# Output projection of an attention + Fourier kernel: the order of the row pairs' splits, of the normalization of the last pairs, and of the first sequence coefficients

## The chip, the cores and the metric

The kernel runs on one core of a Trainium2 chip. The metric is the device time of one execution in microseconds (us); lower is better. The time before is 2464.6 us, the median of three runs (2461.26 to 2467.86).

Five engines of the core work side by side, each through its own list of instructions in a fixed order: TensorE (PE, matrix products; its weight loads are shown apart as PEld), VectorE (DVE), ScalarE (ACT), GpSimd (POOL), and SyncE (SP), which here only issues transfers. An instruction that waits holds up everything behind it on its engine.

## The reference

Two layers, each an attention block followed by a Fourier block, on 2048 rows of 640 numbers, in 32-bit floats:

```python
def _A_ref(x, wqkv, wo):              # H = 32 heads of 20
    qkv = (x @ wqkv) ...
    scores = einsum("bhqd,bhkd->bhqk", q, k) * Dh ** -0.5
    o = einsum("bhqk,bhkd->bhqd", softmax(scores), v)
    return o... @ wo
def _B_ref(x, seq_re, seq_im, hid_re, hid_im):
    a, b = x @ hid_re.T, x @ hid_im.T
    return seq_re @ a - seq_im @ b
x = x + _A_ref(_layernorm(x), wqkv, wo)
x = x + _B_ref(_layernorm(x), ...)
x = x + _A_ref(_layernorm(x), wqkv, wo)
x = x + _B_ref(_layernorm(x), ...)
```

The change lies where `o @ wo` is added to `x` and the result is normalized for the Fourier block. This stage runs twice, once in each layer.

## The kernel before

To keep 32-bit accuracy, every operand of a product is split into a high part (a copy in a rounded format) and a low part (the rest), and a product is three matmuls: high times high, high times low, low times high (`three`, lines 95 to 97). `split` (lines 87 to 90) makes the parts: the high one on ACT (line 89) or DVE (line 87), then the low one on DVE (line 90), which needs the high one.

The projection is `Project.run`. It goes over eight **pairs** p = 0 to 7; a pair is two tiles of 128 rows whose positions are 1024 rows apart. For each pair:

- `load(p + 3)` brings the rows of x for a later pair through the SP queue; a buffer of these is free again when the store of the pair four before it has finished.
- `product(n)` for both tiles: on PE two halves of 320 columns, each of five blocks of three matmuls, so 60 matmuls for a pair, into four PSUM banks that are used in turn. DVE adds x to each half and takes the row sums (line 1006), which frees the bank. The first five tiles have their first three blocks done earlier, during attention.
- after pairs 1 and 3, `fetch` brings the attention output `o` (high and low) of the next four tiles: eight transfers on the SP queue (line 975).
- `normal(k)` for an earlier pair k (the table `LAG`): DVE writes `fold` (line 1061), out of `g` and `na`; `na` comes from ACT (`scale`, lines 1047 to 1049), where the table `SCALED` may put it ahead. For k = 2, 3, 6 and 7 the fold is added to and subtracted from that of k - 2 (line 1066), and the two results are split into `xn` (line 89 on ACT, line 90 on DVE). `xn` numbers 0 to 3 (q) are what the Fourier products read.
- `moments(p)`: the store of the pair to memory (line 1018, SP), the mean (lines 1021 and 1022, POOL), two sums of squares (line 1024, ACT), the power and the factors (lines 1026 to 1041, POOL; line 1040 writes the `nb` that `scale` needs), and `g`, the sum and difference of the two halves of a row (lines 1035 and 1036, DVE).

`normal` is a generator: it stops once after the sums of line 1066, then the run puts `moments(p)` in, and only then do the splits into `xn` follow. So ACT has `scale` of pair 3 and the squares of pair 4 in its list before the high part of xn 0.

The **Fourier products** (`accumulate`) follow with no other work between on PE: q = 0 and 1 for the first two accumulators, then q = 2, then q = 3. They read `xn` and `chl`, the split sequence coefficients. `parts(i)` splits block i of these: high on ACT (line 1209), low on DVE (line 1211). Six blocks are split during the projection, two each after pairs 3, 4 and 5. When both blocks of a load are split, the next load of coefficients (`craw`, line 1201) is issued on SP.

The order of every engine's list is the order in which the code calls these functions; nothing reorders it. POOL's and SP's lists are given by the same calls.

Of the kernel before, what the change touches and what calls it, by code (L numbers as in the profile page):

```python
# [5 lines left out]
F32 = mybir.dt.float32  # L6
# [9 lines left out]
S, D, H, DH = 2048, 640, 32, 20  # L16
# [8 lines left out]
NP = NT // 2  # L25
NQ = NT // 4
LATE = (1, 4, 6)
DONE = 3
LAG = {0: [], 1: [], 2: [0], 3: [1], 4: [2], 5: [3], 6: [4, 5]}
SCALED = {2: [1], 3: [2], 4: [3], 5: [4]}  # L30
FIRST = (0, 1, 4, 5)
HD = D // 2
TOL = 2.0 ** -32
# [5 lines left out]
def mha_fnet_kernel(ctx, tc, x_in, wqk, wv, wo, seq, hid, nat_seq, nat_hid, out):  # L39
# [44 lines left out]
    def split(hl_h, hl_l, src, vector=False):  # L84

        if vector:
            V.tensor_copy(hl_h, src)  # L87
        else:
            A.activation(hl_h, src, AF.Copy)
        V.tensor_tensor(hl_l, src, hl_h.bitcast(F32), op=OP.subtract)  # L90
# [852 lines left out]
    class Project:  # L943
# [105 lines left out]
            A.activation(dst[:, HD + 1:], g[:, HD + 1:], AF.Identity, scale=r, bias=zero[:dst.shape[0]])  # L1049

        def scale(s, p):
            a = s.na[p] = s.next.late("raw1" if p == 1 else "raw0", [D], F32, "na")
            s.scaled(a, s.g[p][:, 0], s.rs[p][:, 0, 0:1], s.nb[p][:, 0:1], s.nb[p][:, 1:2])

        def normal(s, p):
            if p not in s.na:
                s.scale(p)
            rs, g, nb, a = s.rs[p], s.g[p], s.nb[p], s.na[p]
            f = s.f[p] = s.room(f"f{p % 4}", [D], F32, "fold")
            for cols, r in ((slice(0, HD + 1), rs[:, 0, 1:2]), (slice(HD + 1, D), nb[:, 2:3])):  # L1060
                V.scalar_tensor_tensor(f[:, cols], g[:, 1, cols], r, a[:, cols], op0=OP.mult, op1=OP.add)
            if p - 2 not in FIRST:
                return
            q, t = FIRST.index(p - 2), (s.next.late("raw1", [D], F32, "fold2"), f)
            for k, op in enumerate((OP.add, OP.subtract)):
                V.tensor_tensor(t[k], s.f[p - 2], f, op=op)
            yield
            for k in range(2):
                xn = s.next.keep(f"xn{2 * q + k}", [2, D], F32R, "xn")
                s.xn[q, k] = [xn[:, 0], xn[:, 1]]  # L1070
                split(xn[:, 0], xn[:, 1], t[k])

        def run(s):
            s.ot[2] += s.heads(s.room, 2, (1,))
            s.ot.append(s.heads(s.room, 3))
            for m, part in ((0, 1), (1, 0), (1, 1)):
                s.fetch(1, m, part)
            for p in range(NP):
                if p:
                    s.load(p + 3)  # L1080
                for n in (2 * p, 2 * p + 1):
                    s.product(n)
                if p in (1, 3):
                    for m in range(2):
                        for part in range(2):
                            s.fetch(p // 2 + 2, m, part)

                parts = iter(())
                for k in LAG.get(p, [p - 1]):
                    list(parts)  # L1090
                    parts = s.normal(k)
                    next(parts, None)
                if p == 3:
                    s.next.ahead(1, (0,))
                for k in SCALED.get(p, []):
                    s.scale(k)
                s.moments(p)
                list(parts)
                if p == 3:
                    s.next.edge_sum(0)  # L1100
                    s.next.ahead(1, (1,))
                if p == 6:
                    s.next.edge_sum(1)
                    s.next.mids()
                if p == 1:
                    s.next.ahead(0)
                elif p in (4, 5):
                    s.next.ahead(p - 2)
            list(s.normal(NP - 1))

# [4 lines left out]
    class Fourier:  # L1117
# [6 lines left out]
        def weights(s, k):  # L1124
# [11 lines left out]
                split(w[:n, 0], w[:n, 1], s.raw["w", k][:n], vector=True)  # L1136

            return load, parts

        def ahead(s, n, *halves):  # L1140

            for k in range(3) if n == 0 else range(2 * n - 2, 2 * n):
                s.parts(k, *halves) if n else s.load(k)

        def edges(s, n):

# [45 lines left out]
        AHEAD = 6  # L1192
# [430 lines left out]
```

## Time and profile before

| what | us |
|---|---|
| median of three runs | 2464.6 |
| the profiled execution, its own time | 2466.32 |
| its span, first to last instruction | 2464.5 |
| PE busy in it | 2432.3 (99%) |
| ACT busy | 2116.3 (86%) |
| DVE busy | 993.8 (40%) |
| POOL busy | 529.9 (21%) |
| mean clock granted to TensorE | 0.996 |

How to read it: PE and ACT are busy in long stretches of attention, where neither is far from full. A busy PE is no proof that it runs at its peak, so short stretches have to be looked at by themselves: the projection of layer 0 lies at 1103 to 1167 us of the span, that of layer 1 at about 2324 to 2388 us. "Idle before, releaser" in the listings is how long an engine stood still before an instruction and what ended this. The granted clock is the share of TensorE's full clock in a stretch.

### The profile page before, as it was taken

The page shows a single profiled execution, that of the slowest core. Times are in us where ns is not written, and L with a number is a line of the kernel's source. Part 1 is how long each engine was busy: PE and PEld are TensorE (multiplying, and loading weights), DVE is VectorE, ACT ScalarE, POOL GpSimd, SP SyncE. Part 2 cuts the span into 40 slices and gives each one's busy share as a digit, 9 for nine tenths or more (in the row PEclk, how much of TensorE's full clock was granted, in tenths as well). Part 3 has the DMA queues.
Part 4 walks back from the last instruction along what each step waited for, and adds up shares of the span by engine and source line. Part 5 has one row for each costly group of instructions (what it writes and reads, how often), then busy time and mean ns, then how long its engine had stood idle before and what let it go on. Part 6 is the DMA issues. An engine that isn't in the chain of part 4 may idle for free. (4 is left out here: it accounts for less than half of the span.)

```text
span 2464.5 us, 43830 instructions
## 1 busy us (share of the span) xinstructions
PE 2432.3 (99%) x16350; PEld 1178.2 (48%) x16350; DVE 993.8 (40%) x2198; ACT 2116.3 (86%) x2428; POOL 529.9 (21%) x1032
## 2 busy tenths in 40 slices
PE   8999999999999999999999999999999999999998
PEld 7644444443333333349885444454433333333586
DVE  6244442234343333427763444323333232333275
ACT  6699998899999999985457989888999999999752
POOL 2012211112111212114421212211212212222143
PEclk9999999999999999999999999999999999999999
DMA  5224231223222225317552332312221222152265
GB/s 183 100 89 126 81 112 53 77 67 116 72 93 87 96 78 172 93 52 273 189 185 96 111 101 88 114 53 69 82 81 57 92 64 70 55 148 82 81 227 196
DMA packets 128228, 262.64 MB, mean 107 GB/s; under 512 B 29937, under 2 KB 54289, under 8 KB 128005
## 3 DMA queue, kind: packets, MB, share of 16 engines
q1 hardware_dynamic: 89412, 159.89, 20.1%
q0 software_dynamic: 38592, 99.85, 12.7%
q8 instruction: 132, 2.16, 0.4%
q14 instruction: 92, 0.75, 0.1%
HBM read 175.29 MB, written 84.31 MB: 105 GB/s over the span
## 5 line engine op out<-in xcount | busy, mean ns | idle before, releaser
L524 ACT ACTIVATE e<-psc 128x1024 f32<-128x1024 f32 x2048 | 1919.3, 1058 | 110.4 <-PE psc L521 98.7
L532 PE MATMUL acc<-e,v 128*32 128x512 f32 x8192 | 1034.1, 600 | 0.4 <-DVE of L539 0.4
L521 PE MATMUL psc<-stq,stk 62*128 62x512 f32 x4096 | 745.5, 445 | 2.3 <-ACT e L524 1.1
L521 PEld LDWEIGHTS psc<-stq,stk 62*128 62x128 f32 x4096 | 333.5, 184 | 704.0 <-ACT e L524 565.2
L532 PEld LDWEIGHTS acc<-e,v 128*32 128x32 f32 x8192 | 217.4, 108 | 397.0 <-issue 358.6
L102 PE MATMUL pqk<-xt,wqk 128*128 128x512 f32 x1200 | 319.5, 407 | 0.0
L553 POOL DMA_DIRECT2D o<-oh x256 | 131.4, 522 | 827.4 <-DVE oh L548 815.7
L87 DVE CAST hl<-pqk 128x512 fp32r<-128x512 f32 x64 | 44.3, 692 | 597.7 <-PE pqk L102 597.7
L102 PEld LDWEIGHTS pqk<-xt,wqk 128*128 128x128 f32 x1200 | 213.6, 188 | 83.5 <-issue 39.8
L102 PE MATMUL pv<-wv,xt 128*128 128x320 f32 x960 | 151.3, 313 | 0.0
L102 PEld LDWEIGHTS pv<-wv,xt 128*128 128x128 f32 x960 | 141.1, 188 | 15.5 <-issue 9.7
L553 POOL DMA_DIRECT2D o<-ot x256 | 128.4, 509 | 1.6 <-issue 0.8
L539 DVE STREAM_TRANSPOSE of<-acc 128x512 f32<-128x512 f32 x64 | 45.8, 715 | 198.2 <-PE acc L532 198.2
L210 POOL DMA_DIRECT2D scrq<-hl x40 | 28.3, 707 | 429.6 <-DVE hl L90 239.8
L210 POOL DMA_DIRECT2D scrk<-hl x40 | 27.8, 694 | 390.3 <-DVE hl L90 280.8
L95 PE MATMUL py<-wo,o 128*128 128x320 f32 x320 | 103.3, 323 | 8.4 <-DVE xr L1006 8.4
L216 DVE TENSOR_REDUCE top<-pn 32x1 f32<-32x512 f32 x80 | 53.5, 676 | 121.1 <-PE pn L215 120.7
L802 DVE TENSOR_REDUCE far<-cq 128x1 f32<-128x512 f32 (+5 forms) x169 | 98.5, 584 | 5.7
L96 PE MATMUL py<-wo,o 128*128 128x320 f32 x320 | 100.3, 313 | 0.0
L97 PE MATMUL py<-wo,o 128*128 128x320 f32 x320 | 100.3, 313 | 0.0
L806 DVE TENSOR_TENSOR cq<-cq 128x512 f32<-128x512 f32 (+4 forms) x166 | 96.3, 580 | 3.7 <-DMA cq<-in_nat_seq_dram 2.7
L246 DVE COPY v<-pv 128x320 f32<-128x320 f32 x32 | 15.7, 489 | 161.3 <-PE pv L102 161.3
(201 smaller groups left out, 1755.1 us busy)
## 6 DMA issues: line engine op xcount, KB each, us to landing
cq<-in_nat_seq_dram POOLq DMA_DIRECT2D x64, 512.0 KB, 5.3
scrq<-hl POOLq DMA_DIRECT2D x40, 512.0 KB, 3.2
scrk<-hl POOLq DMA_DIRECT2D x40, 512.0 KB, 3.1
stq<-scrq SPq DMA_DIRECT2D x256, 80.0 KB
stk<-scrk SPq DMA_DIRECT2D x128, 160.0 KB
o<-o SPq DMA_DIRECT2D x32, 384.0 KB
stq<-scrq SPq DMA_DIRECT2D x256, 40.0 KB
stk<-scrk SPq DMA_DIRECT2D x128, 80.0 KB
```

The lines of the kernel that those rows point to most:

```text
L95: PE.matmul(out_ap, ah, bh, start=start, stop=False)
L96: PE.matmul(out_ap, ah, bl, start=False, stop=False)
L97: PE.matmul(out_ap, al, bh, start=False, stop=stop)
L102: yield lambda i=i, j=j, k=k: PE.matmul(out_ap, a[i], b[j], start=dc == 0 and k == 0, stop=dc == ND - 1 and k == 2)
L210: G.dma_start(s.scr["qk"[k]][c * 128:(c + 1) * 128, :, tb * 512:(tb + 1) * 512], hl.bitcast(F32))
L216: V.tensor_reduce(s.top[:H, c // ND, c % ND, tb:tb + 1], p, op=OP.max, axis=AX.X)
L521: PE.matmul(p[:, i], s.k[g, kc // 8, j][r, kc % 8 * 128:(kc % 8 + 1) * 128], s.q[g, qb, j][r], start=True, stop=True)
L524: A.activation(e, p, AF.Exp, scale=SCALE)
L532: PE.matmul(s.acc[32 * j:32 * j + 32], s.a.v[kc][:, v0:v0 + 32], s.e[n, j // 2][:, j % 2], start=kc == 0, stop=kc == NT - 1, skip_group_ch ...
L553: G.dma_start(s.o[k, h * DH:(h + 1) * DH, qb * 512:(qb + 1) * 512], hl[k][32 * j:32 * j + DH])
L802: V.tensor_reduce(to, x, op=OP.max, axis=AX.X, apply_absolute_value=True)
L806: V.tensor_tensor(y, x, y, op=op)
```

## The change

The splits into `xn` now follow straight behind the sums of line 1066; `normal` is a plain function. Every pair from 2 on is normalized two pairs later (`LAG`: pair 4 behind the product of pair 6, pair 5 behind that of pair 7), and pairs 6 and 7 follow together at the end. `na` is made one pair ahead for pairs 1 to 6 (`SCALED`), pair 6's in the other of two buffers. The splits of the coefficient blocks stand in a table, `AHEAD`: blocks 0 and 1 at pair 3, 2 and 3 at pair 4, 4 at pair 5, 5 at pair 6, with the high parts always ahead of `scale` and `moments` and the low parts behind.

```diff
-LAG = {0: [], 1: [], 2: [0], 3: [1], 4: [2], 5: [3], 6: [4, 5]}
-SCALED = {2: [1], 3: [2], 4: [3], 5: [4]}
+LAG = {0: [], 1: [], 2: [0], 3: [1], 4: [2], 5: [3], 6: [4], 7: [5]}
+SCALED = {2: [1], 3: [2], 4: [3], 5: [4], 6: [5], 7: [6]}
+AHEAD = {3: (0, 1), 4: (2, 3), 5: (4,), 6: (5,)}
...
-            a = s.na[p] = s.next.late("raw1" if p == 1 else "raw0", [D], F32, "na")
+            a = s.na[p] = s.next.late("raw1" if p in (1, 6) else "raw0", [D], F32, "na")
...
                 V.tensor_tensor(t[k], s.f[p - 2], f, op=op)
-            yield
             for k in range(2):
...
-                parts = iter(())
                 for k in LAG.get(p, [p - 1]):
-                    list(parts)
-                    parts = s.normal(k)
-                    next(parts, None)
-                if p == 3:
-                    s.next.ahead(1, (0,))
+                    s.normal(k)
+                if p in AHEAD:
+                    for i in AHEAD[p]:
+                        s.next.parts(i, (0,))
                 for k in SCALED.get(p, []):
                     s.scale(k)
                 s.moments(p)
-                list(parts)
+                if p == 1:
+                    for _ in range(3):
+                        s.next.load(_)
                 if p == 3:
                     s.next.edge_sum(0)
-                    s.next.ahead(1, (1,))
+                if p in AHEAD:
+                    for i in AHEAD[p]:
+                        s.next.parts(i, (1,))
                 if p == 6:
                     s.next.edge_sum(1)
                     s.next.mids()
-                if p == 1:
-                    s.next.ahead(0)
-                elif p in (4, 5):
-                    s.next.ahead(p - 2)
-            list(s.normal(NP - 1))
+            for k in (NP - 2, NP - 1):
+                s.normal(k)
```

(`ahead`, a helper that called `load` and `parts`, is removed with it.) The lists of PE, SP and POOL stay the same in their order. Those of ACT and DVE change in the projection alone, in the same way in both layers. Line numbers of the changed kernel are one higher up to `normal` and six lower behind `run`; the names are the same.

ACT, behind pair 3's squares (`xsq`) and the sum at the row's edge (`e`), before:

```order
L1178 ACTIVATE e_11361<-c3raw 1x640
L1047 ACTIVATE na<-g,nb,ars 128x321
L1048 ACTIVATE na<-g,nb,ars 128x2
L1049 ACTIVATE na<-g,zero,ars 128x319
L1024 ACTIVATE xsq,sumsq<-xr,mean 128x640 x2
L89 ACTIVATE xn<-fold_11722 128x640
L89 ACTIVATE xn<-fold 128x640
L1209 ACTIVATE chl<-craw 128x512 x2
```

The same place in the changed kernel:

```order
L1172 ACTIVATE e_11361<-c3raw 1x640
L90 ACTIVATE xn<-fold_11722 128x640
L90 ACTIVATE xn<-fold 128x640
L1203 ACTIVATE chl<-craw 128x512 x2
L1048 ACTIVATE na<-g,nb,ars 128x321
L1049 ACTIVATE na<-g,nb,ars 128x2
L1050 ACTIVATE na<-g,zero,ars 128x319
L1025 ACTIVATE xsq,sumsq<-xr,mean 128x640 x2
```

The high parts of xn 0 and the two coefficient blocks moved ahead of pair 3's `na` and pair 4's squares.

DVE from the sums of pair 4's products to those of pair 5's, before:

```order
L1006 SCALAR_TENSOR_TENSOR xr,rowsum<-py,xr 128x320 x4
L1061 SCALAR_TENSOR_TENSOR fold<-g,ars,na 128x321
L1061 SCALAR_TENSOR_TENSOR fold<-g,nb,na 128x319
L1066 TENSOR_TENSOR fold_11722<-fold 128x640
L1066 TENSOR_TENSOR fold<-fold 128x640
L1035 TENSOR_TENSOR g<-xr 128x2x319
L1036 TENSOR_TENSOR g<-xr 128x2x319
L90 TENSOR_TENSOR xn<-fold_11722,xn 128x640
L90 TENSOR_TENSOR xn<-fold,xn 128x640
L1211 TENSOR_TENSOR chl<-craw,chl 128x512 x2
L1006 SCALAR_TENSOR_TENSOR xr,rowsum<-py,xr 128x320 x4
```

The same in the changed kernel:

```order
L1007 SCALAR_TENSOR_TENSOR xr,rowsum<-py,xr 128x320 x4
L1062 SCALAR_TENSOR_TENSOR fold<-g,ars,na 128x321
L1062 SCALAR_TENSOR_TENSOR fold<-g,nb,na 128x319
L1067 TENSOR_TENSOR fold_11722<-fold 128x640
L1067 TENSOR_TENSOR fold<-fold 128x640
L91 TENSOR_TENSOR xn<-fold_11722,xn 128x640
L91 TENSOR_TENSOR xn<-fold,xn 128x640
L1036 TENSOR_TENSOR g<-xr 128x2x319
L1037 TENSOR_TENSOR g<-xr 128x2x319
L1205 TENSOR_TENSOR chl<-craw,chl 128x512 x2
L1007 SCALAR_TENSOR_TENSOR xr,rowsum<-py,xr 128x320 x4
```

The low parts of xn 0 moved ahead of `g`; the same instructions stand between the two sets of sums.

DVE at the end of the projection, behind the sums of pair 7's products; before:

```order
L1061 SCALAR_TENSOR_TENSOR fold<-g,ars,na 128x321
L1061 SCALAR_TENSOR_TENSOR fold<-g,nb,na 128x319
L1066 TENSOR_TENSOR fold_12059<-fold 128x640
L1066 TENSOR_TENSOR fold<-fold 128x640
L1035 TENSOR_TENSOR g<-xr 128x2x319
L1036 TENSOR_TENSOR g<-xr 128x2x319
L90 TENSOR_TENSOR xn<-fold_12059,xn 128x640
L90 TENSOR_TENSOR xn<-fold,xn 128x640
```

The same in the changed kernel:

```order
L1062 SCALAR_TENSOR_TENSOR fold<-g,ars,na 128x321
L1062 SCALAR_TENSOR_TENSOR fold<-g,nb,na 128x319
L1036 TENSOR_TENSOR g<-xr 128x2x319
L1037 TENSOR_TENSOR g<-xr 128x2x319
L1062 SCALAR_TENSOR_TENSOR fold<-g,ars,na 128x321
L1062 SCALAR_TENSOR_TENSOR fold<-g,nb,na 128x319
L1067 TENSOR_TENSOR fold_12080<-fold 128x640
L1067 TENSOR_TENSOR fold<-fold 128x640
L91 TENSOR_TENSOR xn<-fold_12080,xn 128x640
L91 TENSOR_TENSOR xn<-fold,xn 128x640
```

The first fold here was pair 6's and is now pair 5's; pair 6's fold, its sums and xn 2 stand behind pair 7's `g`. Pair 7's fold and xn 3 close both lists.

More of the change, by code (lines that the diff above doesn't have):

```diff
@@ L1138, in weights @@
             return load, parts
-        def ahead(s, n, *halves):
-            for k in range(3) if n == 0 else range(2 * n - 2, 2 * n):
-                s.parts(k, *halves) if n else s.load(k)
         def edges(s, n):
```

## The prediction

> **What bounds the kernel now.** I first read the list of waits of PE, since PE and ACT carry the span and the change touches ACT and DVE only where PE runs dense products. It gives, for PE, who was waited for: us in total, times, longest.
>
> ```profile
> PE ptr L166 <- ACT xa L129: 8.7, 2, 8.3
> PE py L95 <- DVE xr L1006: 8.4, 4, 3.5
> ```
>
> Apart from the start (8.3), the only wait of weight in the program is that for line 1006, which frees the projection's PSUM banks. The timeline of PE puts it at the first product of pair 6 in both layers (start, length, what, idle before):
>
> ```profile
> 1107.80 0.41 PE L95 MATMUL py<-wo,o 128*128 128x320 f32 x1 [0.67 <-DVE xr L1006]
> ...
> 1147.68 0.57 PE L95 MATMUL py<-wo,o 128*128 128x320 f32 x1 [3.53 <-DVE xr L1006]
> 1166.92 0.40 PE L95 MATMUL pacc<-chl,xn 128*128 128x512 f32 x1
> ...
> 2367.91 0.63 PE L95 MATMUL py<-wo,o 128*128 128x320 f32 x1 [3.53 <-DVE xr L1006]
> 2387.96 0.40 PE L95 MATMUL pacc<-chl,xn 128*128 128x512 f32 x1
> ```
>
> PE stands still from 1144.15 to 1147.68, and from 2364.38 to 2367.91. The `pacc` rows are the first Fourier products; call their start F. A second loss hides in "busy". At full speed two matmuls are 0.147 us apart: 89 steps lie between these two rows, (1132.84 - 1119.78) / 89.
>
> ```profile
> 1119.78 0.31 PE L95 MATMUL py<-wo,o 128*128 128x320 f32 x1
> ...
> 1132.84 0.31 PE L97 MATMUL py<-wo,o 128*128 128x320 f32 x1
> ```
>
> So the 120 matmuls of pairs 6 and 7 need 17.6 us. They took 1166.92 - 1147.68 = 19.24 in layer 0 and 20.05 in layer 1: 1.64 and 2.45 too many. The table of short stretches says why; behind the counts of the engines stands the granted clock, then the DMA share and GB/s:
>
> ```profile
> 1108.00:1109.00 1.00, 1.00 (x8) 1.00 (x8) 0.98 (x6) 0.00 (x0) 1.00 (x3) 1.00 0.79 249
> 1147.00:1148.00 1.00, 0.32 (x1) 0.32 (x2) 1.00 (x6) 0.00 (x0) 0.47 (x2) 0.89 0.91 247
> 1151.00:1152.00 1.00, 1.00 (x8) 1.00 (x8) 1.00 (x2) 1.00 (x2) 0.00 (x0) 0.91 0.98 398
> 2366.00:2367.00 1.00, 0.00 (x0) 0.00 (x0) 1.00 (x3) 0.31 (x1) 0.91 (x3) 0.67 1.02 321
> 2373.00:2374.00 1.00, 1.00 (x8) 1.00 (x7) 0.20 (x1) 1.00 (x3) 0.34 (x2) 0.92 0.21 86
> ```
>
> The first row, behind the idle 0.67, is at full clock. Read as shares of full and half clock, the others put the fall at 1147.78 and the return at about 1151.2, and in layer 1 the fall at 2366.34 and the return at 2373.2. Half the cold time with work in it is 1.7 and 2.6, which fits the excess. The stall thus costs 3.53 + 1.64 = 5.17 in layer 0 and 3.53 + 2.45 = 5.98 in layer 1: **11.15 us together**.
>
> Why line 1006 was late is read on DVE, ACT and POOL before it:
>
> ```profile
> 1140.14 0.22 POOL L1040 TENSOR_SCALAR nb<-nb 128x1 f32<-128x1 f32 x1
> ...
> 1140.40 0.66 ACT L1047 ACTIVATE na<-g,nb,ars 128x321 f32<-128x321 f32 x1 [3.55 <-POOL nb L1040]
> 1143.70 1.35 ACT L89 ACTIVATE xn<-fold 128x640 fp32r<-128x640 f32 x2
> ...
> 1136.85 1.69 DVE L1066 TENSOR_TENSOR fold<-fold 128x640 f32<-128x640 f32 x2
> 1138.45 0.82 DVE L1035 TENSOR_TENSOR g<-xr 128x638 f32<-128x638 f32 x1
> 1144.45 1.56 DVE L90 TENSOR_TENSOR xn<-fold,xn 128x640 fp32r<-128x640 f32 x2 [4.45 <-ACT xn L89]
> 1145.93 1.29 DVE L1211 TENSOR_TENSOR chl<-craw,chl 128x512 fp32r<-128x512 f32 x2
> 1147.14 0.48 DVE L1006 SCALAR_TENSOR_TENSOR xr<-py,xr 128x320 f32<-128x320 f32 x1
> ```
>
> ACT idles 3.55 us for POOL's `nb` of pair 3, then does `na` and the squares, and only then the high part of xn 0, whose sum DVE had finished at 1138.54. DVE, in order, idles 4.45 for it, with pair 5's line 1006 behind.
>
> **The change part by part.** *Splits behind the sums, pair 4.* The same instructions, nothing added; only their place differs. The high parts can start when the first sum is done, 1137.7, in time that ACT spends idle; 1.35 us later they are done, and the two blocks of `chl` (1.13 before) by 1140.4, when `nb` comes, so `na` and the squares keep their times. DVE: low parts 1138.5 to 1140.2 (1.69 as for xn 3 below, one behind each high part), `g` 1.55 to 1141.8, `chl` 1.29 to 1143.0. Line 1006 of pair 5 starts at 1143.0 instead of 1147.14, and its bank is free at 1143.5, ahead of the end of pair 5's products at 1144.15. The stall's cause is gone with 0.6 us in hand: gain up to 11.15, and without the stall the clock has no reason to fall.
>
> *What is late next: the transfers of `o`.* Pair 6 is the first to read the `o` that line 975 fetches after pair 3. That queue is unchanged and does not move earlier with PE (SP's timeline; sizes of its transfers; three stretches with the GB/s last; the first reader of a later load):
>
> ```profile
> 1138.22 0.37 SPq L996 DMA_DIRECT2D xr<-in_x_dram x1
> 1138.68 4.87 SPq L975 DMA_DIRECT2D o<-o x8
> ...
> o<-o SPq DMA_DIRECT2D x10, 384.0 KB
> o<-o SPq DMA_DIRECT2D x12, 256.0 KB
> xr<-in_x_dram SPq DMA_DIRECT2D x4, 640.0 KB
> craw<-in_seq_dram SPq DMA_DIRECT2D x5, 512.0 KB
> ...
> 1139.00:1144.00 5.00, 5.00 (x36) 4.88 (x34) 1.00 (x2) 3.54 (x8) 1.95 (x7) 1.00 0.95 292
> 2360.00:2365.00 5.00, 4.38 (x30) 4.11 (x29) 0.55 (x2) 4.31 (x9) 1.87 (x7) 1.00 1.00 312
> 1180.00:1183.00 3.00, 3.00 (x20) 2.73 (x19) 1.93 (x4) 0.76 (x2) 0.00 (x0) 1.00 0.59 186
> 1183.91 1.15 ACT L1209 ACTIVATE chl<-craw 128x512 fp32r<-128x512 f32 x2 [3.15 <-DMA craw<-in_seq_dram]
> ```
>
> The load of `xr` (640 KB, 0.655 MB) stands first; then come 384 KB of high and 384 KB of low `o`, 1.44 MB in all. At 292 GB/s from 1139 that has moved by 1143.95, at 312 from 2360 by 2364.67. How long after its last byte a load releases its reader I take from the coefficient load at 1183.91: 0.524 MB at 186 GB/s from 1180 have moved by 1182.9, so 1.0 us. Low `o` is there at 1144.95 and 2365.67; the third matmul of pair 6 would be due at 1144.45 and 2364.68 (0.3 behind the first). New waits: 0.5 and 1.0, and by the same sum 0.1 and 0.2 for the next 512 KB nine matmuls later. **Price 1.8 us**. Bounds: no lag at all gives 0, two us of lag 1.8 + 4 × 0.5 = 3.8; I take 1.0, the one measured lag.
>
> Does a rest of 0.6 to 1.2 us drop the clock? The nearest rows: the idle 0.67 at 1107.80 is followed by a clock of 1.00, and in layer 1 the clock fell after 2364.38 to 2366.34, 1.95 of idling. 1.2 lies between, nearer to the first, so I take nothing; the bounds are nothing and 1.64 + 2.45 = 4.1. [...]
>
> *Pairs 4 to 6 two behind, coefficient blocks spread.* Pair 5's DVE work loses one block's low part (0.69 of the 1.29) and pair 6's loses one fold (1.1) and gains that block; at most 8.8 - 0.6 = 8.2 us of work in pair 5 (four sums 1.64, folds 1.1, sums 1.69, `g` 1.55, low parts 1.56, blocks 1.29 before) against 8.8 of PE for a pair (60 × 0.147). DVE stays ahead; cost nothing. Block 5's high part now waits for its load ahead of pair 5's `na`; the load follows `o` and a store, 4.45 MB, about 1154 by the rates above, and pair 5's `nb` comes later (squares at about 1152, plus POOL's 3.2 as below). Nothing.
>
> *The last two together.* Here the change adds order: xn 2 stands behind pair 7's `g`, and POOL's copy into that `g` waits for fold 5. The rows of before:
>
> ```profile
> 1170.63 0.42 POOL L1026 TENSOR_SCALAR sumsq<-sumsq 128x2 f32<-128x2 f32 x1 [1.99 <-ACT xsq L1024]
> 1173.64 0.22 POOL L1040 TENSOR_SCALAR nb<-nb 128x1 f32<-128x1 f32 x1
> 1177.85 1.69 DVE L90 TENSOR_TENSOR xn<-fold,xn 128x640 fp32r<-128x640 f32 x2
> ...
> 1175.30 0.40 PE L95 MATMUL pacc<-chl,xn 128*128 128x512 f32 x1
> 1182.15 0.40 PE L95 MATMUL pacc<-chl,xn 128*128 128x512 f32 x1
> ```
>
> xn 2 is first read at 1175.30 = F + 8.4, xn 3 at 1182.15 = F + 15.2. Behind pair 7's last sums (F + 0.7) DVE has fold 5 (1.0), `g` (1.55), fold 6 (1.0), sums (1.65), low parts (1.7): xn 2 at F + 7.6, 0.8 early. xn 3 hangs on POOL's chain, 3.2 us from the first row above to the second, then `na`, fold, sums and splits: F + 12.6 before (1179.54), and the same now, since xn 2's high parts on ACT end at F + 6.6, before `nb`. 2.6 early. Cost nothing, as long as these margins hold.
>
> **Sum.** 11.15 - 1.8 = 9.35 us. The profiled execution took 2466.32, so 2456.97; the median of the runs is 1.72 lower, which gives **2455.3 us**, 0.38% faster. Everything behind F is PE-bound up to the next prologue and moves along.
>
> **Rivals.**
> 1. *Nothing is left over*: `o` lands in time. For it: before, no wait for it is seen, but it was covered by 3.53. Time 2464.6 - 11.15 = 2453.4.
> 2. *The rest is longer, or drops the clock*: 3.8 us of waits, or 1.8 with the fall in one or both layers. Times 2457.3, and 2457 to 2459.4.
> 3. *The wait only moves*: DVE is not through by 1144.15 (its margin is 0.6). Every us beyond costs one in each layer; at 4.1 the change does not do what it says, 2464.6.
> 4. *Slower: xn 3 comes late.* POOL's chain of pair 7 now runs under DVE's fold 6 and sums, and POOL's small operations are seen stretched:
>
> ```profile
> L1040 POOL TENSOR_SCALAR nb<-nb x8: 209/383/802, 1117.7 to 1173.6; 128x1 f32<-128x1 f32 x8
> ```
>
> With 0.6 us more on lines 1034, 1039 and 1040 each, xn 3 comes 1.8 later: still 0.8 early. It decides only from 2.6 us on. Then a stall d costs d and, from 1.95 up, about 2 us of clock; break-even is d = 2.7 in each layer, and d = 5 gives 2455.3 + 2 × 7 = 2469. [...]
>
> **How the numbers follow.** My forecast 0.50, rival 1 0.15, rival 2 0.20, rival 3 0.10, rival 4 0.05. The runs of before spread 3.3 us to each side, their median less. The range of 8 in 10: from rival 1 less 1.9 for spread, 2451.5, to rival 2's 2459.4 plus 2, 2461.5. About 0.3% (7.4 us) can be told from no change: faster than 2457.2 takes most of the forecast (0.43), rival 1 (0.14) and some of rival 2 (0.04): 0.61. Slower by as much is part of rival 4 alone: 0.03. Within: 0.36.
>
> **What would show it.** Right: line 90's idle of 4.45 gone, its work ahead of line 1035, pair 5's first line 1006 near 1143; at pair 6 no wait for DVE but one of 0.5 to 1.2 on `o`; clock 1.00 through the projection; F 4.6 us earlier in layer 0 and 9.35 in layer 1, and no wait at 8.4 or 15.2 behind F. Wrong: a wait of more than 2 us still at pair 6, whatever its releaser, a clock below 1.00, or a wait of `pacc` on line 89 or 90.

## The result and the profile after

| | before | changed |
|---|---|---|
| median of 17 runs each | 2464.93 us | 2460.17 us |
| lowest to highest | 2461.26 to 2467.86 | 2456.64 to 2464.69 |
| profiled execution | 2466.32 | 2460.17 |
| its span | 2464.5 | 2458.3 |
| granted clock over the span | 0.996 | 0.998 |

The ratio is 0.998, with a 95% interval of 0.9972 to 0.9987: some 4.8 us faster, about half of what was predicted, and within the range.

PE's list of waits in the changed kernel (who was waited for: us in total, times, longest) has 1.3 for line 1006 (now 1007) instead of 8.4, and holds new names beside it. Its lines are one higher than before up to the projection, six lower behind it.

```profile
PE pacc L96 <- DVE u L91: 1.4, 1, 1.4
PE py L96 <- DVE xr L1007: 1.3, 2, 0.7
...
PE py L98 <- DMA o<-o: 1.0, 2, 0.5
PE py L96 <- DVE fold L1062: 1.0, 1, 1.0
PE pturn L1253 <- DVE c3raw L1245: 0.9, 1, 0.9
```

The timeline of PE puts them in place (start, length, what, and in brackets the idle time before it):

```profile
1107.33 0.42 PE L96 MATMUL py<-wo,o 128*128 128x320 f32 x1 [0.67 <-DVE xr L1007]
1144.67 0.39 PE L96 MATMUL py<-wo,o 128*128 128x320 f32 x1 [0.99 <-DVE fold L1062]
1145.71 0.41 PE L98 MATMUL py<-wo,o 128*128 128x320 f32 x1 [0.50 <-DMA o<-o]
1163.31 0.40 PE L96 MATMUL pacc<-chl,xn 128*128 128x512 f32 x1
...
2324.47 0.42 PE L96 MATMUL py<-wo,o 128*128 128x320 f32 x1 [0.67 <-DVE xr L1007]
2361.61 0.41 PE L98 MATMUL py<-wo,o 128*128 128x320 f32 x1 [0.51 <-DMA o<-o]
2379.20 0.40 PE L96 MATMUL pacc<-chl,xn 128*128 128x512 f32 x1
2402.16 0.50 PE L96 MATMUL pacc<-chl,xn 128*128 128x512 f32 x1 [1.44 <-DVE u L91]
2407.47 1.25 PE L1253 MATMUL pturn<-one,c3raw 1*128 1x1 f32 x12 [0.86 <-DVE c3raw L1245]
```

Three things are to be seen. Pair 6 no longer stalls for 3.53 us; in layer 0 it waits 0.99 and 0.50, in layer 1 0.51. The 0.99 is put down to a fold on DVE, which this product does not read; an experiment below shows that it too is `o`. And behind layer 1's projection stand two waits, 1.44 and 0.86, that before did not have at all. From F in layer 1 (the first `pacc`) to the end of the span the changed kernel takes 2458.3 - 2379.20 = 79.10 us, before 2464.5 - 2387.96 = 76.54: **2.56 us are given back there.**

The chain that the change was made for, on ACT and then DVE, in layer 0:

```profile
1137.23 1.60 ACT L90 ACTIVATE xn<-fold 128x640 fp32r<-128x640 f32 x2 [1.13 <-DVE fold L1067]
1138.74 1.14 ACT L1203 ACTIVATE chl<-craw 128x512 fp32r<-128x512 f32 x2
1139.78 0.64 ACT L1048 ACTIVATE na<-g,nb,ars 128x321 f32<-128x321 f32 x1
...
1138.01 1.69 DVE L91 TENSOR_TENSOR xn<-fold,xn 128x640 fp32r<-128x640 f32 x2
1139.61 0.82 DVE L1036 TENSOR_TENSOR g<-xr 128x638 f32<-128x638 f32 x1
...
1141.08 1.29 DVE L1205 TENSOR_TENSOR chl<-craw,chl 128x512 fp32r<-128x512 f32 x2
1142.28 0.48 DVE L1007 SCALAR_TENSOR_TENSOR xr<-py,xr 128x320 f32<-128x320 f32 x1
```

The splits and the coefficient copies fill most of the time in which ACT had idled 3.55 us for `nb`; DVE has no gap, and pair 5's sums begin at 1142.28, not at 1147.14. In the table of short stretches the clock (the number before the DMA share and the GB/s) stays whole where it had stood at 0.89 and 0.67:

```profile
1147.00:1148.00 1.00, 1.00 (x7) 0.80 (x7) 0.97 (x2) 1.00 (x2) 0.91 (x2) 1.00 1.06 334
2366.00:2367.00 1.00, 1.00 (x9) 1.00 (x8) 1.00 (x2) 1.00 (x3) 0.00 (x0) 1.00 1.08 409
```

### The profile page after: what moved, and what is told of

It reads as the page before. It is cut to its first block, busy times and chain, and to the rows that moved or that the text cites. A ratio compares the mean times of both kernels' runs of the same rounds, so it can differ in the third digit from the quotient of the medians.

```text
span 2458.3 us, 43836 instructions
## 1 busy us (share of the span) xinstructions
PE 2428.5 (99%) x16350; PEld 1174.1 (48%) x16350; DVE 995.3 (40%) x2198; ACT 2117.6 (86%) x2428; POOL 527.7 (21%) x1032
```

## The experiments

Each ran beside before on the same chip: e0 to e3 on one, where before's median was 2465.54 us (28 runs), e4 to e7 on a second (2465.76, 21 runs), e8 and e9 on a third (2465.33, 11 runs). Ratios are to before on that chip. Four stretches are read from each profile with the same two rows: the projection of a layer, from the product behind the idle 0.67 to F, and what follows F.

| | projection, layer 0 | F to layer 1's projection | projection, layer 1 | F to the end | span |
|---|---|---|---|---|---|
| before | 59.12 | 1161.11 | 59.93 | 76.54 | 2464.5 |
| the change, first profile | 55.98 | 1161.16 | 54.73 | 79.10 | 2458.3 |
| second (e0) | 54.20 | 1160.97 | 56.31 | 77.60 | 2456.7 |
| third (e9) | 55.27 | 1161.14 | 55.60 | 77.90 | 2457.9 |
| e1, splits alone | 57.53 | 1161.69 | 57.54 | 78.44 | 2462.8 |
| e2, all but the splits | 59.12 | 1161.35 | 57.66 | 79.07 | 2465.0 |
| e4, splits and copies | 55.31 | 1162.03 | 54.68 | 79.05 | 2458.8 |
| e5, fetch alone | 59.12 | 1161.30 | 60.31 | 76.56 | 2464.8 |
| e3, change + fetch first | 53.78 | 1161.29 | 53.78 | 77.58 | 2454.1 |
| e6, e3 again | 53.78 | 1161.11 | 53.78 | 77.78 | 2454.1 |
| e7, e3 + copy ahead | 53.78 | 1161.71 | 53.78 | 76.44 | 2453.0 |
| e8, change + copy ahead | 55.64 | 1161.05 | 53.79 | 76.53 | 2454.8 |

### e0: the change again

> The changed kernel once more, for a second profile. It asks whether the 2.56 us that the first profile of the change lost between the end of layer 1's projection and the end of the span (79.1 us there against 76.5 before) belongs to the change. Theory 'one slow transfer': the three coefficient loads behind the projection land 3.7 to 4.0 us after their issue in both layers, as in before (3.75 and 3.97), nothing waits for them, and that stretch takes 76.5 to 77. Rival 'the change makes them late': about 6.5 us again in layer 1 and 79 again. On o, both expect the waits at pair 6 again: 0.8 to 1.8 us in layer 0, 0.4 to 1.2 in layer 1. Median within 2 us of 2460.2.

2459.63 us (2456.98 to 2463.41, 11 runs), ratio 0.9979 (0.997 to 0.9988). The waits of layer 1 in this profile, and what came before the second of them, on SP and ACT; the last two rows are before's:

```profile
2359.95 0.38 PE L96 MATMUL py<-wo,o 128*128 128x320 f32 x1 [0.82 <-DMA o<-o]
2361.09 0.41 PE L98 MATMUL py<-wo,o 128*128 128x320 f32 x1 [0.62 <-DMA o<-o]
2405.81 1.25 PE L1253 MATMUL pturn<-one,c3raw 1*128 1x1 f32 x12 [0.87 <-DVE c3raw L1245]
...
2392.98 2.13 SPq L1195 DMA_DIRECT2D craw<-in_seq_dram  x3
2397.89 1.15 ACT L1203 ACTIVATE chl<-craw 128x512 fp32r<-128x512 f32 x2 [4.31 <-DMA craw<-in_seq_dram]
```

```profile
2401.18 2.14 SPq L1201 DMA_DIRECT2D craw<-in_seq_dram  x3
2405.15 1.15 ACT L1209 ACTIVATE chl<-craw 128x512 fp32r<-128x512 f32 x2 [3.37 <-DMA craw<-in_seq_dram]
```

Neither theory held as written, and on `o` the expectation missed too (the projections lie 0.42 and 2.53 above the 53.78 that e3 takes without such waits). The first coefficient load did not take 6.46 us as in the first profile (2393.08 to 2399.54), and the 1.44 that hung on it is gone: that wait depends on the execution (e4, below, has it too, with a load of 5.72). But the wait of 0.86 came again, with a load of 4.91 us (before: 3.97). Against F, the loads go out 13.88 us behind it now, 13.22 before, and ACT can read the first at 18.79, not 17.19. Wherever the first load can be read later than 18.9 behind F, the wait on `u` is what exceeds this: 1.44 at 20.34 and 20.35 (first profile, e4), 0.74 at 19.65 (e1), none at 18.90 (e3). DVE takes its work in order, so the copies' low parts, the splits `u` and then `c3raw` come that much later, and PE waits for the last.

Of the 1.6 us, 0.66 is the change's own order. Pair 7's small operations on POOL now run beside xn 2's low parts on DVE. POOL and DVE in this profile, and POOL in before's:

```profile
2384.91 1.70 DVE L91 TENSOR_TENSOR xn<-fold,xn 128x640 fp32r<-128x640 f32 x2
...
2384.96 0.83 POOL L1035 COPY g<-xr 128x4 f32<-128x4 f32 x1
...
2386.03 0.67 POOL L1041 TENSOR_SCALAR nb<-nb 128x1 f32<-128x1 f32 x1
```

```profile
2394.24 0.19 POOL L1034 COPY g<-xr 128x4 f32<-128x4 f32 x1
...
2394.67 0.22 POOL L1040 TENSOR_SCALAR nb<-nb 128x1 f32<-128x1 f32 x1
```

The copy takes 0.83 instead of 0.19 and `nb` 0.67 instead of 0.22, so pair 7's `na`, xn 3, the copies behind it and the loads that these set free are 0.66 later (`na` at F + 7.63, before F + 6.97). In before the copy starts at 2394.24, where xn 2's low parts end on DVE (2392.69, 1.55 long); that the work on DVE is what stretches POOL's is my estimate from these rows. The other 0.94 is the load itself; why it took longer stays open.

### e1 and e2: which half of the change does it

e1 is before with the generator taken out, so that the splits stand behind their sums:

```diff
                 V.tensor_tensor(t[k], s.f[p - 2], f, op=op)
-            yield
             for k in range(2):
...
-                parts = iter(())
                 for k in LAG.get(p, [p - 1]):
-                    list(parts)
-                    parts = s.normal(k)
-                    next(parts, None)
+                    s.normal(k)
...
                 s.moments(p)
-                list(parts)
...
-            list(s.normal(NP - 1))
+            s.normal(NP - 1)
```

> Before with the splits of a row tile right behind its sum, and nothing else of the change. My theory (the low part of row tile 0 stood behind the next pair's moments and held the vector engine 4.45 us): the stall of 3.53 us ahead of pair 6 and the half clock behind it are gone in both layers, what is left there is the wait on o, and the time is that of the whole change within 1.5 us. Rival (the longer lag and the coefficient copies moved back free ScalarE, not the place of the splits): a stall of over 2 us ahead of pair 6 stays in both layers, and the time is within 1.5 us of before.

e2 is the change with exactly these lines put back.

> The change with the splits put back behind the moments: the lag of two pairs to the end, the last two together and the coefficient copies ahead stay. My theory: the stall ahead of pair 6 stays (3 to 4 us each layer, with the half clock behind it), and the time is within 1.5 us of before, 2463.5 to 2466. Rival (lag and copies bring the gain): no stall ahead of pair 6, and 4 to 5 us less than before.

e1: 2465.59 us (2464.55 to 2467.12, 11 runs), ratio 1.0001 (0.9992 to 1.001): **no gain**. My theory, as put, fell, and what its rival named as signs came: a stall of over 2 us at pair 6 in both layers (2.10 and 2.09), and the time of before. PE, then DVE and ACT ahead of its first wait, in e1:

```profile
1146.04 0.42 PE L95 MATMUL py<-wo,o 128*128 128x320 f32 x1 [2.10 <-DVE xr L1006]
1156.23 0.42 PE L95 MATMUL py<-wo,o 128*128 128x320 f32 x1 [1.13 <-DVE xr L1006]
...
1144.28 1.29 DVE L1206 TENSOR_TENSOR chl<-craw,chl 128x512 fp32r<-128x512 f32 x2 [2.83 <-ACT chl L1204]
...
1140.09 0.66 ACT L1047 ACTIVATE na<-g,nb,ars 128x321 f32<-128x321 f32 x1 [0.99 <-POOL nb L1040]
1143.63 1.14 ACT L1204 ACTIVATE chl<-craw 128x512 fp32r<-128x512 f32 x2
```

The wait moved on down DVE's list. DVE no longer stands at xn 0's low part but, 2.83 us long, at the low parts of the two coefficient blocks, whose high parts still come behind `na` and the squares on ACT. The same happens once more at pair 7 (1.13). In the profile the two projections are 4.0 us shorter than before's, since no half clock follows its stalls (right behind those of 2.10 and 1.13 in layer 0 the products start 0.15 us apart, where in before at half clock it was 0.27), but 1.9 of it is lost again behind F, and the timed runs show none of the rest. Why they don't is not settled: the profiled execution is the fastest of the eleven, with a granted clock of 0.999, and eight of the other ten have a lower one (0.996 to 0.998), as a half clock behind these stalls would give; but one run at 0.999 took 2466.76.

e2: 2468.78 us (2465.04 to 2471.64, 11 runs), ratio 1.0012 (1.0003 to 1.0021). The stall stays, as expected, and the rival (that the lag and the copies bring the gain) falls; that the kernel is about 3 us slower than before was not expected. Its profile in layer 1, PE first, then the granted clock in stretches:

```profile
2368.14 0.41 PE L96 MATMUL py<-wo,o 128*128 128x320 f32 x1 [3.53 <-DVE xr L1007]
2412.72 1.25 PE L1258 MATMUL pturn<-one,c3raw 1*128 1x1 f32 x12 [0.86 <-DVE c3raw L1250]
```

```profile
2368.14:2385.93 17.79, 17.79 (x121) 17.71 (x122) 14.91 (x38) 9.73 (x20) 6.50 (x18) 1.00 0.80 289
...
2414.00:2415.00 1.00, 1.00 (x3) 0.81 (x4) 0.49 (x3) 0.51 (x3) 0.00 (x0) 0.56 1.04 394
2415.00:2416.00 1.00, 1.00 (x3) 0.76 (x3) 0.47 (x3) 0.36 (x3) 0.00 (x0) 0.50 0.38 141
...
2417.00:2418.00 1.00, 1.00 (x6) 0.67 (x5) 0.00 (x0) 0.00 (x0) 0.00 (x0) 0.74 0.00 0
```

The stall is the same 3.53 as in before, but this time, in layer 1, no half clock follows (1.00 up to F, and a projection of 57.66 instead of 59.93). It comes later: the wait of 0.86 stands in this kernel too, and behind it the clock is half from 2414.12 to 2417.52, which costs half of 3.4, 1.7 us. 76.54 + 0.86 + 1.7 = 79.10, where 79.07 was measured. The profiled execution is only 0.4 us slower than before's (2466.76 against 2466.32) and doesn't show where the 3 us go. Its granted clock is 0.997; the four runs with that clock have a median of 2466.4, the seven at 0.995 or 0.996 one of 2469.1. A half clock behind the stall in both layers and behind the 0.86 would fit these; no timeline of such a run shows it.

### e4: splits and copies, without the longer lag

```diff
-LAG = {0: [], 1: [], 2: [0], 3: [1], 4: [2], 5: [3], 6: [4], 7: [5]}
-SCALED = {2: [1], 3: [2], 4: [3], 5: [4], 6: [5], 7: [6]}
+LAG = {0: [], 1: [], 2: [0], 3: [1], 4: [2], 5: [3], 6: [4, 5]}
+SCALED = {2: [1], 3: [2], 4: [3], 5: [4]}
...
-            for k in (NP - 2, NP - 1):
-                s.normal(k)
+            s.normal(NP - 1)
```

(against the change; pair 6's `na` is back in its buffer of before.)

> The change with the lag, the scaling and the end of before: only the splits behind their sums and the coefficient copies ahead of the scaling stay. Theory A (the splits alone moved the vector engine's wait to the coefficients' low parts, 2.83 us on the coefficient copies of ScalarE in the third profile, and the copies put ahead free it): no wait of pair 6 or 7 on a sum over 0.3 us, only the waits on o, and within 1.5 us of the whole change's 2460. Theory B (the lag of two pairs to the end is needed too): a stall of over 1 us on a sum at pair 6 or 7 in both layers, and 2463 or more.

2460.64 us (2458.62 to 2465.34, 11 runs), ratio 0.9981 (0.9972 to 0.999); at pair 6 only waits on `o` (0.53 in layer 0, 0.58 in layer 1), and at pair 7 none. Theory A holds: the splits and the copies' high parts ahead of `na` are the gain. Neither is one alone: e1 has the splits without the copies ahead, e2 the copies (with the lag) without the splits. The lag of two pairs to the end, scaling ahead and the last two together add nothing that 11 runs can tell.

The loss behind the projection is there too, though the last two pairs are not put together. SP and then ACT in e4, layer 1, where F is 2379.75:

```profile
2394.38 2.13 SPq L1194 DMA_DIRECT2D craw<-in_seq_dram  x3
...
2400.10 1.15 ACT L1202 ACTIVATE chl<-craw 128x512 fp32r<-128x512 f32 x2 [5.12 <-DMA craw<-in_seq_dram]
```

The loads go out 14.63 us behind F (e1: 14.47; the change: 13.88; before: 13.22), and the waits of 1.44 and 0.86 follow, in layer 0 one of 0.65. With before's end and the splits behind their sums, as in e1 and e4, xn 2's low parts stand ahead of pair 7's `g` on DVE; POOL's copy into `g` is not stretched (0.19) but starts later, at F + 7.66 in layer 0 of e4, before at F + 6.29.

### e3, e5 and e6: what `o` waits for

SP's list of waits in layer 0's projection of the change, and its rows there:

```profile
SPq L997 <- DMA d_x<-xr: 25.9, 4, 8.2
```

```profile
1139.11 0.37 SPq L997 DMA_DIRECT2D xr<-in_x_dram  x1
1139.57 4.91 SPq L976 DMA_DIRECT2D o<-o  x8
```

The residual load of pair 6 goes into the buffer of pair 2 and stands on SP until pair 2's store has landed; the fetch of `o` stands behind it, though the row tiles that it overwrites first have been read by then. e3 exchanges the two:

```diff
-                if p:
+                if p and p != 3:
                     s.load(p + 3)
...
                             s.fetch(p // 2 + 2, m, part)
+                if p == 3:
+                    s.load(p + 3)
```

> The change, with the load of pair 6's residual rows put behind the fetch of the last o tiles on SP instead of ahead of it. Theory: the fetch is late because SP stands at that load until pair 2's store has landed (the waits on the store come to 25.9 and 24.2 us in the two projections); freed of it, the fetch starts some 8 us earlier in layer 0 (at about 1131 instead of 1139.6), no product of pair 6 waits for o, and the time is 2 to 3 us below the whole change's. Rival: the store's own bytes and the loads share the DMA engines, so the transfers end no earlier, the waits on o stay over 1 us in layer 0, or the residual rows come late in their place; no gain over the change within 0.7 us.

e5 makes the same edit in before:

> Before, with the load of pair 6's residual rows behind the fetch of the last o tiles on SP, and nothing else. Theory: in before the o tiles land while TensorE waits for the sum anyway, so the stall of 3.53 us at pair 6 stays in both layers and the time is within 1 us of before. Rival: the fetch sets part of that stall; then it shrinks by over 0.5 us in each layer and the time by over 1.5.

e6 is e3 again, beside e7:

> The change with the fetch ahead of the residual load once more, beside the next one. 2456 to 2458; no wait at pair 6; one wait of 0.86 us at the turn of the middle row in layer 1 (on the vector engine), and 77.6 us from the end of layer 1's projection to the end of the span, as in its first profile.

e3: 2456.90 us (2455.91 to 2458.97, 6 runs), ratio 0.9966 (0.9954 to 0.9979); e6: 2456.09 us (2455.84 to 2457.3, 5 runs), ratio 0.9963 (0.9949 to 0.9976). SP and PE in e3:

```profile
1130.84 0.41 SPq L1019 DMA_DIRECT2D d_x<-xr  x1
1131.35 9.26 SPq L976 DMA_DIRECT2D o<-o  x8
1140.78 0.59 SPq L997 DMA_DIRECT2D xr<-in_x_dram  x1
```

```profile
1107.67 0.42 PE L96 MATMUL py<-wo,o 128*128 128x320 f32 x1 [0.68 <-DVE xr L1007]
...
1161.45 0.40 PE L96 MATMUL pacc<-chl,xn 128*128 128x512 f32 x1
```

The median is 2.7 below the change's on the same chip (e0), as expected; the two intervals overlap, but the profile shows the cause. The fetch starts 8.2 us earlier, and no product of pair 6 waits, not even the one whose wait had been put down to a fold: it was `o`. Both layers' projections take 53.78, to the hundredth, and again in e6, which also has the one wait of 0.86 that was expected. So the change's waits on `o` cost 2.20 + 0.95 = 3.15 us in its first profile, 0.42 + 2.53 = 2.95 in the second and 1.49 + 1.82 = 3.31 in the third.

e5: 2466.15 us (2462.19 to 2467.62, 11 runs), ratio 0.9998 (0.9989 to 1.0007), with the stall of 3.54 in both layers. While DVE was late, the late `o` cost nothing.

### e7 and e8: what was given back

Against e3 (e7) and against the change (e8), the first accumulation is written ahead of pair 7's normalization, with the next coefficient copy behind it:

```diff
-            for k in (NP - 2, NP - 1):
-                s.normal(k)
+            s.normal(NP - 2)
+            if s.first:
+                s.next.acc = {}
+                s.next.accumulate(s.next.ORDER[0])
+                s.next.parts(s.next.AHEAD)
+            s.normal(NP - 1)
```

(the Fourier stage's loop skips these two; `first` is set in the program's main branch.)

> The same with the first accumulation of the Fourier stage written ahead of the last pair's normalization, and behind it the next coefficient copy, so that the first of the three coefficient loads is issued some 5 us earlier (at about 8 us behind the end of the projection, not 13.9). Theory: the wait of 0.86 us at the turn of the middle row comes from that load (it landed 18.9 us behind the end of the projection where before had 17.2); the wait is gone, the stretch from the end of layer 1's projection takes about 76.6 us instead of 77.6, and the time is about 1 us lower, 2455 to 2456.5. Rival: the load isn't what holds the vector engine there; the wait stays, and the time is within 0.5 us of the kernel beside it; or the copy delays row tile 3 and a wait of over 0.3 us on it appears.

> The change with the first accumulation and the next coefficient copy ahead of the last pair's normalization, but with the residual load ahead of the fetch as in the change. Theory (two separate losses, o at pair 6 and the coefficient load behind the projection): the waits on o stay (the two projections take 1 to 3.5 us more together than 2 times 53.78), the stretch behind layer 1's projection takes 76.4 to 76.6 us, no wait for the sums of u or the middle row there; the median is 1 to 2.5 us below the change's beside it, and the runs still spread by over 4 us. Rival (both losses come from the same late SP queue): the stretch stays at 77.6 or more as long as o is late, and the time is within 0.7 us of the change.

> The change a third time, beside the last one: 2458 to 2462, waits on o of 0.4 to 3 us in the two projections together, and 77.6 to 79.1 us behind layer 1's projection.

e7: **2455.15 us** (2454.81 to 2456.14, 5 runs), ratio 0.9957 (0.9944 to 0.9971), the fastest of all, 10.6 us below before and 0.9 below e6 beside it, as expected (the intervals of e6 and e7 overlap). e8: 2457.41 us (2456.27 to 2459.63, 6 runs), ratio 0.9968 (0.9956 to 0.9981). e9, the change beside it: 2458.95 us (2456.04 to 2461.61, 6 runs), ratio 0.9972 (0.996 to 0.9984). ACT and SP in e7, layer 1, where F is 2376.56:

```profile
2383.10 0.62 ACT L1209 ACTIVATE chl<-craw 128x512 fp32r<-128x512 f32 x1
...
2384.70 7.28 SPq L1201 DMA_DIRECT2D craw<-in_seq_dram  x3
```

The first load goes out 8.14 us behind F, not 13.88, and no wait over 0.25 us is left in that stage; F to the end takes 76.44 in e7 and 76.53 in e8, as in before. In e8 the waits on `o` remain (1.86 in layer 0 above 53.78, 0.01 in layer 1). The two losses are separate. The median of e8 is 1.5 below e9's, as expected, but with six runs each it is not told apart by itself. That e8's runs would still spread by over 4 us was a miss: they spread by 3.4.

## Why the prediction came out as it did

*The stall and its size.* Predicted as worth 11.15 us. Both projections without any wait (e3) take 59.12 + 59.93 - 2 × 53.78 = 11.49 less. Right in place, cause and size.

*Splits behind the sums.* Right: the work was to end with pair 5's sums at 1143.0, and they came at 1142.28 (the layer began 0.47 earlier). The step had moved the coefficient blocks together with the splits without saying that both were needed. e1 shows that they are: with the splits alone, the wait moves on and nothing is gained.

*The transfers of `o`.* The right next wait, in the right place, but **1.8 was too small**: 3.15 in the same profile, 2.95 and 3.31 in the others; inside the bounds 0 to 3.8. The step took the start of SP's queue as given ("unchanged and does not move earlier"). It does not move earlier, but it is not fixed: the load at its head waits for a store to land, and went out at 1139.11 instead of 1138.22. That it was the head of the queue which set the time, and not the bytes, is shown by e3.

*The clock.* Right: no rest of up to 1.56 us on `o` at pair 6 (that one in e9, with a clock of 1.00 in every stretch from 2362 to 2440) was followed by a lower clock in any profile.

*The last two together, "cost nothing".* xn 3 was in time, as said. Here the prediction failed all the same: it followed xn 2 and xn 3 to their readers and stopped. Behind xn 3 on ACT and DVE stand the coefficient copies that set free the next three loads, and their slack was smaller than xn 3's. "Everything behind F is PE-bound up to the next prologue and moves along" was therefore wrong for layer 1: 2.56 us in the first profile, 1.06 and 1.36 in the next two. Rival 4 had put a price on POOL's small operations coming late under DVE's sums, but with xn 3 as its victim, at a threshold of 2.6; 0.66, with a load that took 0.94 longer, sufficed elsewhere. It is not the new end alone that makes the loads late: e1 and e4, with before's end, load later still (14.47 and 14.63 behind F against 13.88). What failed is that xn 2 and xn 3 were followed to their readers and the loads were not. e7 and e8 show it, since they bring the load forward and the loss is gone.

*The sum.* For the profiled execution: predicted 2456.97, measured 2460.17. The difference of 3.20 is 1.35 from `o` and 2.56 from behind F, less 0.34 by which the stall was worth more, and 0.37 from an earlier start of the first projection and rounding. No rival priced the loss behind F. The range ended at rival 2's slowest time, 2459.4, plus 2 us for spread, and the measured median of 2460.17 lies inside it only by these 2 us; that part was luck.

*From the profiled execution to the median.* I took 1.72 off, as for before; over 17 runs of before it is 1.39. The changed kernel's profiled execution lay on its median. Before's profile had a half clock behind both stalls, and e2 shows the same 3.53 without one, so that the 1.72 may have been a clock that most runs of before do not lose twice; it then belonged to the stall and went with it. The granted clock on record for each run points that way: of the 60 runs of before beside the experiments, 26 at 0.996, the clock of the profiled execution, have a median of 2466.3, 26 at 0.997 one of 2465.0, and seven at 0.998 one of 2464.15. It is argued, not shown: the unprofiled runs carry no timeline that says where the clock fell.

*The spread* was not foreseen. The change's 17 runs lie within 8.1 us of each other; with `o` early (e3 and e6, 11 runs) it is 3.1, and with the coefficient load early too (e7, 5 runs) 1.3; with that load alone early (e8, 6 runs) 3.4. Fewer runs spread less by themselves, but six of the change (e9) had 5.6. The wider spread goes with the transfers that the change uncovered; that it comes from them is not shown.

## What to carry to other kernels

An in-order engine that waits for another gives up that wait only when everything between it and the late result has moved: ask, for each instruction behind the one that is freed, whose result it needs next (e1, where DVE's wait of 4.45 us came back as one of 2.83). When a stall goes, what it had covered is paid: look at the queues that did not get earlier with it, and at what stands at their head rather than at their bytes alone (e3, against e5). And follow a delayed chain past its next reader, to the loads that it sets free; the slack there may be smaller than the one that you checked.

## What the runs showed of the hardware

The same idle time of 3.53 us was followed by half clock in both layers of before and in e2's layer 0, and by none in e2's layer 1 (1.00 from 2368.14 to 2385.93), while an idle 0.86 with twelve 1x1 products behind it was followed by 3.4 us of half clock in that run and by none in the change's three profiles.

So the length of a pause alone does not decide. Read from the table of short stretches, the clock fell at 1147.78 and 2366.34 in before and stayed half for 3.4 and 6.8 us (0.50 in each whole slice between); in e2 it fell in layer 1 at 2414.12, to 0.50 as well, for 3.4. In before the fall of layer 0 came 3.63 us behind the start of the stall (1144.15), 0.10 after PE had started again, and that of layer 1 came 1.96 us behind it (2364.38), 1.57 before PE started again. Ahead of the fall at 2414.12 in e2 lie the idle 0.86 and the twelve small products, 2.1 together. What decides beside the length was not shown.

Of the three coefficient loads, 512 KB each, issued together behind an idle stretch of the queue, the first could be read 3.97 us after their issue in before's layer 1, 4.91 in e0 and 6.46 in the change's first profile. It is not chance from run to run alone: in layer 1 it took 3.97 in before and 3.65 in e5, and 4.91 to 6.46 in the eight profiles whose loads went out 13.88 us or more behind F; in layer 0 of all ten it took 3.40 to 3.82. What made the difference was not settled.
